# A two-dimensional FFT with a routed eight-expert network on one core: the order of the first thirteen steps and of the first weights

## The chip, the cores and the metric

The kernel runs on one core of a Trainium2 chip. The metric is the device time of one execution in microseconds (us). The engines are called PE (TensorE, matmuls), DVE (VectorE), ACT (ScalarE), POOL (GpSimd) and SP (SyncE, which issues most DMAs).

## The reference

```python
def _attn_ref(x):                       # x: 8 x 2496 x 256
    X = np.fft.fft(x, axis=1)
    X = np.fft.fft(X, axis=2)
    return X.real.astype(np.float32)

def _moe_ref(x, w_gate, w_output_gate, w1, w2):      # x: 19968 x 256, 8 experts, 256 -> 1024 -> 256
    logits = x @ w_gate
    e_idx = np.argmax(logits, axis=1)
...
    gate_w = probs[np.arange(N), e_idx]
    eom = 1.0 / (1.0 + np.exp(-(x @ w_output_gate)))
...
        h = np.maximum(x[mask] @ w1[e], 0.0)
        ye = h @ w2[e]
        out[mask] = gate_w[mask, None] * eom[mask, e, None] * ye
```

The real part of a two-dimensional FFT of each of 8 batches gives 19968 tokens of 256 numbers. Each token goes to the one of eight experts with the largest logit, through two matrix products with a ReLU between, and is scaled by two gates.

## The kernel before, in words

**FFT.** A batch comes in five chunks of 128 x 1024 floats (`xt`, 512 KB each, `load_x`, L302). `fold1` (L413) adds the two halves of a chunk; for batches from 3 on it makes two more half folds (L416, L417). `fold2` (L429, L432, L441, L443) makes sums and differences of the parts and frees the chunk, which starts the next `xt` load; ACT squares the result for the batch's energy (L451). `energy`, `energy_sum` and `scale` (L454 to L467, with the helper at L270) make a power of two from it. `dstage` (L482 to L486) is the first matrix product, in float32, five per batch. `devac` brings its result from PSUM as two half-precision parts, the high one on ACT (`ahi`, L494), the low one on DVE (`alo`, L495). The second product, `sstage` (L521), comes in five steps of 24, 24, 60, 36 and 36 matmuls per batch, so there are 40 steps n = 5b + i. `sevac` (L536 to L556) turns a step's result into rows of tokens: `qb`, `qs`, `eo`, `rt`, `rows`.

**Routing.** `gating(b)` is a generator in pieces "C" and "A" that computes logits, the expert and the destination of each token (`desti`), and then scatters the batch's rows to the buffer `scr` in memory with 20 indirect DMAs on POOL (L653). It yields after scatters 4, 9 and 14 (`SPL`), so that other POOL work comes between. `table_a(0)` makes the table of which expert serves which slot, for the tokens of batches 0 and 1 (`BAS[0]` = 2).

**Weights' scales.** 16 loads of 1 MB (`wt`, L363, two buffers) are squared on ACT (L367), summed by PE (L371), and give scales (`wscales`, and `ssc`, L715 to L717 per slot).

**Experts.** A slot is 256 tokens. `load_x_` reads its rows from `scr`, transposed (`xr`, L1075) and their two gates (`xf`, L1076). `load_w` reads its expert's weights as float32 halves (`raw0b`, `raw1b`, L1089); `conv` splits each into a high part on ACT (L1095) and a low part on DVE (L1096) and then issues the reload of that `raw` buffer for the next block. PE makes `hp` (L1115), ACT `hh` (L1119) and DVE `hl` (L1120) split it again, PE makes `yp` (L1135), ACT scales it (`y`, L1142), and POOL scatters it to the output (L1143).

**Order.** `start()` and `steps()` are the FFT's program. Up to step `FSTART` = 15 the program runs under `manual_schedule(engines=PH1)`: SP and POOL keep the written order, and a scheduler orders PE, DVE and ACT. Then the pools of the experts are opened, `table_a(0)` is made, and expert slots and the further FFT steps are interleaved (`rates`, `work`), in the same mode. Only the last part is fully in written order. A queue is served in order: an instruction that waits holds up all behind it on its engine.

## Time and profile before

| what | value |
|---|---|
| runs of the kernel before | 1174.66 us median of 3 (1174.36, 1174.66, 2767.52) |
| the profiled execution, own time | 1159.36 us |
| its span in the profile | 1157.5 us |
| its mean granted PE clock | 0.973 |
| PE busy, share of the span | 1052.7 us, 91% |
| DVE busy | 833.0 us, 72% |
| ACT busy | 731.6 us, 63% |
| POOL busy | 498.6 us, 43% |

The profile shows one execution; its times count from the start of the span. A row of the timeline gives start and duration in us, engine, line, operation, what is written from what, and in brackets the idle time before it and what ended it. A row of waits gives who waited for whom: us in total, how often, the longest. A row of groups gives a line's busy time, the mean of one in ns, and the idle time before it. A row of the stretches gives length and then busy time and instructions of PE, PEld (weight loads), DVE, ACT and POOL, the granted PE clock, the DMA engines' share and GB/s.

### The profile page before, as it was taken

What the parts mean: (1) busy time and instruction counts of PE and PEld (TensorE: products, weight loads), DVE (VectorE), ACT (ScalarE), POOL (GpSimd) and SP (SyncE); (2) the same over time, 40 slices, a digit from 0 to 9 for tenths busy, and PEclk for the clock granted to TensorE, in tenths of its full rate; (3) what the DMA queues carried; (4) which work ended last, traced back from release to release, by engine and by line L of the source; (5) the groups of instructions that cost most, each with busy time, mean ns of one, the idle gap of its engine ahead of it and who ended that gap; (6) DMA issues with size and microseconds to landing.
All of it is one profiled execution on the core that took longest, in us unless ns stands there. A gap on an engine that the chain in (4) does not pass through costs nothing.

```text
span 1157.5 us, 28573 instructions
## 1 busy us (share of the span) xinstructions
PE 1052.7 (91%) x10060; PEld 934.4 (81%) x10060; DVE 833.0 (72%) x1535; ACT 731.6 (63%) x1216; POOL 498.6 (43%) x430
## 2 busy tenths in 40 slices
PE   3877469989999999998999999999999989999998
PEld 3666458878788887887878888889989979998887
DVE  7876797878988747568445454588777867787684
ACT  2598657666666654553445454587777767777684
POOL 5418873786577444462564122223222322322231
PEclk9998779999999999999999999999999999999999
DMA  7778554755547545464767524557457464655651
GB/s 285 300 260 346 214 161 137 222 164 149 168 144 183 138 131 151 137 166 143 186 182 177 142 57 122 154 159 196 128 170 201 125 166 113 175 166 147 183 130 30
DMA packets 158213, 194.09 MB, mean 168 GB/s; under 512 B 117885, under 2 KB 118527, under 8 KB 156020
## 3 DMA queue, kind: packets, MB, share of 16 engines
q1 hardware_dynamic: 142100, 149.68, 46.6%
q0 software_dynamic: 15824, 42.14, 10.9%
q8 instruction: 79, 1.29, 0.5%
q14 instruction: 66, 0.54, 0.2%
q10 hardware_dynamic: 144, 0.44, 0.1%
HBM read 193.47 MB, written 43.46 MB: 205 GB/s over the span
## 4 chain that ended last, share of the span: by engine, by line
PE 63%; DVE 11%; issue 8%; POOL 6%; ACT 5%; DMA 3%; SPq 2%; another core or an unknown queue 0%; POOLq 0%; DVEq 0%; ACTq 0%
PE hp L1115 30%; PE yp L1135 29%; PE psb_t L521 3%; POOL scr L653 2%; POOL out_dram L1143 2%; DVE w1b L1096 1%; DVE rt L549 1%; DMA raw1b<-in_w_dram 1%; DVE hl L1120 1%; POOL xt L413 1%; SPq L1057 1%; ACT wt L367 1%; DVE w0b L1096 1%; DVE xt L432 1%; ACT w1b L1095 1%
## 5 line engine op out<-in xcount | busy, mean ns | idle before, releaser
L1115 PE MATMUL hp<-xr,w0b 128*128 128x256 f16 (+2 forms) x4224 | 482.8, 264 | 20.9 <-DVE hl L1120 13.7
L1135 PE MATMUL yp<-w1b,hh 128*128 128x256 f16 x2608 | 450.4, 273 | 6.7 <-issue 3.6
L1143 POOL DMA_INDIRECT out_dram<-y,xf x163 | 214.7, 1317 | 554.1 <-ACT y L1142 520.2
L1115 PEld LDWEIGHTS <-w0b 128*128 128x128 f16 x4224 | 384.6, 98 | 70.4 <-issue 15.4
L1135 PE MATMUL yp<-w1b,hl 128*128 128x256 f16 (+3 forms) x1304 | 356.0, 273 | 2.0 <-issue 2.0
L1135 PEld LDWEIGHTS <-hh 128*128 128x128 f16 x2608 | 251.9, 98 | 40.3 <-issue 11.9
L1119 ACT ACTIVATE hh<-hp 128x512 f16<-128x512 f32 (+4 forms) x352 | 194.0, 554 | 131.6 <-PE hp L1115 112.9
L1120 DVE SCALAR_TENSOR_TENSOR hl<-hp,hh 128x512 f16<-128x512 f32 (+4 forms) x352 | 222.0, 637 | 68.2 <-ACT hh L1119 56.9
L1096 DVE SCALAR_TENSOR_TENSOR w1b<-raw1b,ssc,w1b 128x1024 f16<-128x1024 f32 x144 | 186.3, 1294 | 111.7 <-ACT w1b L1095 90.3
L1096 DVE SCALAR_TENSOR_TENSOR w0b<-raw0b,ssc,w0b 128x1024 f16<-128x1024 f32 x144 | 190.2, 1324 | 69.6 <-ACT w0b L1095 51.7
L653 POOL DMA_INDIRECT scr<-rows,desti x160 | 178.6, 1116 | 73.3 <-issue 43.8
L1095 ACT ACTIVATE w0b<-raw0b,ssc 128x1024 f16<-128x1024 f32 x144 | 164.6, 1146 | 64.6 <-PE hp L1115 28.6
L1095 ACT ACTIVATE w1b<-raw1b,ssc 128x1024 f16<-128x1024 f32 x144 | 165.2, 1148 | 55.0 <-PE yp L1135 25.0
L1135 PEld LDWEIGHTS <-hl 128*128 128x128 f16 (+3 forms) x1304 | 127.9, 98 | 19.0 <-issue 4.2
L1142 ACT ACTIVATE y<-yp,ysc 128x256 f32<-128x256 f32 (+1 forms) x163 | 68.9, 470 | 43.4 <-PE yp L1135 34.2
L413 POOL TENSOR_TENSOR xt<-xt 128x500 f32<-128x500 f32 (+1 forms) x35 | 47.0, 1346 | 21.8 <-DMA xt<-in_xl_dram 19.5
L482 PE MATMUL psb_t<-tdet,ft 128*125 128x290 f32 (+1 forms) x120 | 36.2, 458 | 16.5 <-DVE alo L495 12.2
L482 PEld LDWEIGHTS psb_t<-tdet,ft 128*125 128x125 f32 (+1 forms) x120 | 24.7, 213 | 25.1 <-issue 13.5
L521 PE MATMUL psb_t<-ahi,tstq 125*128 125x145 f16 (+1 forms) x384 | 41.4, 227 | 3.3 <-DVE rt L539 2.0
L521 PEld LDWEIGHTS <-tstq 125*128 125x128 f16 (+1 forms) x576 | 38.6, 97 | 5.4 <-issue 4.6
L551 ACT CAST rows<-rt 128x516 f16<-128x516 f32 x40 | 25.0, 625 | 21.7 <-DVE rt L549 11.3
L484 PE MATMUL psb_t<-tdet,ft 128*125 128x145 f32 (+1 forms) x100 | 22.9, 313 | 16.8 <-DVE alo L495 9.4
(214 smaller groups left out, 916.4 us busy)
## 6 DMA issues: line engine op xcount, KB each, us to landing
raw0b<-in_w_dram SPq DMA_DIRECT2D x144, 512.0 KB
raw1b<-in_w_dram SPq DMA_DIRECT2D x144, 512.0 KB
xt<-in_xl_dram SPq DMA_DIRECT2D x40, 512.0 KB
wt<-in_w_dram SPq DMA_DIRECT2D x16, 1024.0 KB
out_dram<-y,xf POOLq DMA_INDIRECT x163
scr<-rows,desti POOLq DMA_INDIRECT x160
xr<-scr SPq DMA_TRANSPOSE x88
xf<-scr SPq DMA_DIRECT2D x75, 2.0 KB
```

Of the source, the lines that this page charges most:

```text
L413: eng.tensor_tensor(x0, x0, x1, op=ALU.add)
L482: nc.tensor.matmul(o[:, 0:290], ft[:, k, par, W], tdab[:, k], start=(k == 0), stop=(k == 1))
L521: nc.tensor.matmul(ps[:, k, c0:c0 + 145], tab[hl][t][K], a[K, kc, par, c0:c0 + 145], start=(n == 0), stop=(n == len(terms) - 1))
L653: free_order("scr", batch=b, inst=nc.gpsimd.indirect_dma_start(out=scr[:, :], out_offset=bass.IndirectOffsetOnAxis(ap=desti[:, j:j + 1], a ...
L1095: nc.scalar.activation(w[:, 0], r, AF.Copy, scale=sc)
L1096: nc.vector.scalar_tensor_tensor(w[:, 1], r, sc, w[:, 0], op0=ALU.mult, op1=ALU.subtract)
L1115: nc.tensor.matmul(ps[:, k, T], w1v[:, hl, kc, (f % 4) * 128:(f % 4 + 1) * 128], a["x"][:, x, T], start=(m == 0), stop=(m == 5))
L1119: nc.scalar.activation(hh[:, G, T], ps[:, :, T], AF.Relu)
L1120: nc.vector.scalar_tensor_tensor(hl[:, G, T], ps[:, :, T], 0.0, hh[:, G, T], op0=ALU.max, op1=ALU.subtract)
L1135: nc.tensor.matmul(a["yp"][0:M, u], a[k, h][:, f, u * 128:u * 128 + M], w2v[:, hl, f], start=(g == 0 and f == 0 and m == 0), stop=(h == 1 ...
L1142: nc.scalar.activation(a["y"][0:M, u], a["yp"][0:M, u], AF.Copy, scale=ys[0:M, u:u + 1])
L1143: free_order("out", nc.gpsimd.indirect_dma_start(out=out[:, :], out_offset=bass.IndirectOffsetOnAxis(ap=a["f"].bitcast(I32)[0:M, u, 1:2], ...
```

## The change

1. All folds of batches 0 to 2 (`fold1`, `fold2`) run on DVE; before, some ran on POOL.
2. `start()` is in written order on all engines, written anew, with table loads among the x loads; the first two `wt` loads come at its end.
3. The weight squares are spread to end by step 11 instead of 15.
4. At step 10 the whole of `gating(1)` is woven in at once, with its 20 scatters in a row (`SPL` counts only from batch 2 on), and `table_a(0)` up to its scales.
5. `FSTART` is 13 instead of 15. At step 12 the rest of the table is made, the experts' pools are opened, and the first four weight loads and `conv(0, 0, h)` come, with the reloads they issue, ahead of `load_x_(0)`. `hold` keeps batch 4's x loads back until then.
6. Batches 3's and 4's folds come later (`AHEAD`), and batch 3's five `dstage` calls stand at step 14 (`DSTEP`), with later energies (`ESTEP`).

The lines of the kernel change their numbers: fold1 L413 is L420, half folds L416/417 are L423/424, fold2 L429/432/441/443 are L435/438/447/449, `alo` L495 is L502, scatters L653 are L660, `conv` on DVE L1096 is L1128, `xr` L1075 is L1107, the raw loads L1089 are L1121, `hp` L1115 is L1147, `hl` L1120 is L1152.

```diff
@@ -63,11 +63,17 @@
 MARGIN = 2 + len(SPL)
-FSTART = 5 * BA + MARGIN
-W0, NW = 2, 2
-AHEAD = (5, 6, 7, 8, 9), (4, 5, 6, 7, 8)
+MARGIN0 = 3
+FSTART = 5 * BA + MARGIN0
+WEND, NW = FSTART - 1, 2
+AHEAD = {0: (5, 6, 7, 8, 9), BA - 1: (5, 5, 5, 5, 5), BA: (0, 1, 3, 5, 6)}
+AHEAD_ = (2, 4, 5, 5, 6)
+ESTEP = 1, 3, 2
+DSTEP = ((), (), (0, 1), (2, 3), (4,)), ((), (), (), (), (0, 1, 2, 3, 4)), ((), (), (), (0, 1, 2), (3, 4))
@@ -293,7 +299,7 @@
             while n and len(xq) < NB * KC:
-                q = pw if held[pw] < NX2 and len(xq) < FSTART + 8 else px
+                q = pw if held[pw] < NX2 and len(xq) < FSTART + 3 else px
                 if held[q] == (NX2 if q is pw else NX):
@@ -319,7 +325,7 @@
         nc.sync.dma_start(tdot, tdo)
-        load_x()
+        load_x(KC - 1)
@@ -379,6 +385,7 @@
         gens = []
+        first, hold = [], []
@@ -425,11 +432,10 @@
             v = xts[b, c].rearrange("p (h a b) n -> p h a b n", h=2, a=2)[:, h]
-            eng = nc.gpsimd if b < 2 and c in (2, 4) else nc.vector
-            eng.tensor_sub(ft[:, :, 1, W], v[:, :, 0, W], v[:, :, 1, W])
+            nc.vector.tensor_sub(ft[:, :, 1, W], v[:, :, 0, W], v[:, :, 1, W])
             yield
             e = v[:, :, 0]
-            eng.tensor_add(e[:, :, W], e[:, :, W], v[:, :, 1, W])
+            nc.vector.tensor_add(e[:, :, W], e[:, :, W], v[:, :, 1, W])
             if c in (0, 2):
@@ -444,7 +450,8 @@
                 held[xq[b * KC + k]] -= 1
-                load_x()
+                if not hold:
+                    load_x()
                 if b == 0:
@@ -657,7 +664,7 @@
                     scatter(j)
-                    if j in SPL:
+                    if j in SPL and b >= BA:
                         yield "C"
@@ -783,6 +790,7 @@
             yield
+            yield "scales"
             yield from slot_scales(ea, n, i)
@@ -930,52 +938,79 @@
         def start():
             gt_ = gate_tables()
-            next(gt_)
-            for c in range(KC):
-                fold1(0, c, nc.gpsimd if c % 2 else nc.vector)
-                if c == 2:
-                    for _ in gt_:
-                        pass
-                weave(fold2(0, c))
-                if c > 2:
-                    dstage(0, c - 3)
             for j in range(2):
                 load_t(j)
+                load_x(1)
+            def fold(c):
+                weave(fold2(0, c))
+            fold1(0, 0, nc.vector)
+            next(gt_)
+            fold(0)
+            fold1(0, 1, nc.vector)
+            for _ in gt_:
+                pass
+            fold(1)
+            for c in range(2):
+                dstage(0, c)
+            fold1(0, 2, nc.vector)
+            fold(2)
+            fold1(0, 3, nc.vector)
+            fold(3)
+            fold1(0, 4, nc.vector)
+            energy(0)
+            energy_sum(0)
+            dstage(0, 2)
+            for j in range(2, 4):
+                load_t(j)
+            fold(4)
             nc.sync.dma_start(tidt, tid)
                 nc.sync.dma_start(scr[DUM + 128 * k:DUM + 128 * (k + 1), :], ztile)
-            energy(0)
-            energy_sum(0)
+            for j in range(4, 6):
+                load_t(j)
             scale(0)
             for c in range(KC):
-                if c > 1:
-                    dstage(0, c)
                 devac(0, c)
+                if c < 2:
+                    dstage(0, c + 3)
+                if c == 2:
+                    fold1(1, 0, nc.vector)
+            for k in range(NW):
+                wload(k)
             wk = 0
-            fc = KC
+            fc = KC + 1
             for n in range(5 * NB):
                 b, i = divmod(n, 5)
+                late = int(b >= BA) + int(b > BA)
                 if i == 0 and b > 0:
                     add_gen(gating(b - 1))
+                    if b == BA:
+                        hold.append(1)
+                        for ph in "CACC":
+                            weave(piece(ph))
+                        first.append(table_a(0))
+                        while next(first[0]) != "scales":
+                            pass
                 smalls.clear()
-                ds_ = ((), (), (0, 1), (2, 3), (4,))[i] if b + 1 < NB else ()
+                ds_ = DSTEP[late][i] if b + 1 < NB else ()
                 for c in ds_:
                 fillers = [piece("C")]
-                for j in range(2, 6) if n == 0 else ():
-                    load_t(j)
-                while fc <= min(KC * (b + 1) + AHEAD[b >= BA][i], KC + 3 * n + 2):
+                while fc <= min(KC * (b + 1) + AHEAD.get(b, AHEAD_)[i], KC + 3 * n + 2):
                     m = fc
                     if m < NB * KC:
-                        fold1(*divmod(m, KC), nc.vector if m % KC == 1 and m // KC < 3 else nc.gpsimd)
+                        fold1(*divmod(m, KC), nc.vector if m // KC < 3 else nc.gpsimd)
                     if m - 1 < NB * KC and m > KC:
@@ -986,21 +1021,18 @@
                     pass
-                if i == 1 and b + 1 < NB:
+                if i == ESTEP[late] and b + 1 < NB:
                     energy(b + 1)
                 weave(piece("A"))
-                while wk <= 2 * E and wk < (n - W0 + 1) * (2 * E + 1) / (FSTART - W0):
+                while wk <= 2 * E and wk < (n + 1) * (2 * E + 1) / WEND:
                     if wk < 2 * E:
                     wk += 1
-                if n == W0 - 1:
-                    for k in range(NW):
-                        wload(k)
                 yield ("step", n)
@@ -1146,13 +1178,15 @@
         def experts():
-            chained(load_x_, 0)
             for m in range(2):
                     chained(load_w, 0, m, h)
-            chained(load_x_, 1)
             for h in range(2):
                 conv(0, 0, h)
+            yield "w"
+            chained(load_x_, 0)
+            hold.clear()
+            chained(load_x_, 1)
             yield "i"
@@ -1227,31 +1261,36 @@
+    with tc.manual_schedule():
+        start()
     with tc.manual_schedule(engines=PH1):
-        start()
         steps_ = steps()
         for m in steps_:
+            if m == ("step", WEND):
+                for _ in first[0]:
+                    pass
+                rp.close()
+                fx.append(pl(ctx, name="fr", bufs=2, side="right"))
+                add_raw(fx[0])
+                add_wbuf(fx[0])
+                fg = experts()
+                next(fg)
             if m == ("step", FSTART):
                 break
-        rp.close()
-        fx.append(pl(ctx, name="fr", bufs=2, side="right"))
         pps.close()
         pool["m"] = pl(pps, name="psm2", bufs=1, space=PS)
-        for _ in table_a(0):
-            pass
-        add_raw(fx[0])
-        add_wbuf(fx[0])
+        next(fg)
+        load_x()
         bg = background()
         ends = [n - 2 for n in range(1, NS) if sched[n][0] != sched[n - 1][0]]
-        work = [5 * (b - a) + 45 * C_TAB for a, b in zip(BAS, BAS[1:])] + [5 * (NB - BAS[-1]) - MARGIN + 28 * C_SCAT + 50 * C_TAB + 3.5]
+        work = [5 * (b - a) + (MARGIN - MARGIN0) * (i == 0) + 45 * C_TAB for i, (a, b) in enumerate(zip(BAS, BAS[1:]))] + [5 * (NB - BAS[-1]) - MARGIN + 28 * C_SCAT + 50 * C_TAB + 3.5]
         rates = [w / (9.0 * (e - s_)) for w, s_, e in zip(work, [0] + ends, ends)]
         acc, slot = 0.0, 0
-        fg = experts()
         for m in fg:
```

On **POOL**, from the first scatters on. `xt` are chunks, `rows` the tokens' rows of a step, `desti` a batch's destinations (its number tells the batch: the first is batch 0, the second batch 1). Before:

```order
L653 DMA scr_60<-rows_308,desti_791 161024x258 x4
L653 DMA scr_60<-rows_375,desti_791 161024x258
L413 TENSOR_TENSOR xt_496<-xt_496 128x4x125
L416 TENSOR_TENSOR xt_496<-xt_496 128x2x125
L417 TENSOR_TENSOR xt_496<-xt_496 128x2x125
L653 DMA scr_60<-rows_375,desti_791 161024x258 x3
L653 DMA scr_60<-rows_500,desti_791 161024x258 x2
L413 TENSOR_TENSOR xt_639<-xt_639 128x512
L416 TENSOR_TENSOR xt_639<-xt_639 128x256
L417 TENSOR_TENSOR xt_639<-xt_639 128x256
L653 DMA scr_60<-rows_500,desti_791 161024x258 x2
```

Of the change:

```order
L660 DMA scr_60<-rows_659,desti_794 161024x258 x4
L660 DMA scr_60<-rows_733,desti_1162 161024x258 x4
L660 DMA scr_60<-rows_796,desti_1162 161024x258 x4
L660 DMA scr_60<-rows_978,desti_1162 161024x258 x4
L660 DMA scr_60<-rows_1046,desti_1162 161024x258 x4
L660 DMA scr_60<-rows_1107,desti_1162 161024x258 x4
L420 TENSOR_TENSOR xt_384<-xt_384 128x4x125
L423 TENSOR_TENSOR xt_384<-xt_384 128x2x125
```

All 40 scatters of batches 0 and 1 stand in a row, and the folds of batch 3 (`xt_384`, `xt_504`, `xt_508`) and of batch 4's first chunks, which stood between them, stand behind.

On **DVE**, around the first conversion of weights (`w0b00`, `w0b01` are the two halves of the first product's weights). Before:

```order
L443 TENSOR_TENSOR ft_2654<-xt_1123,xt_1264 128x2x125
L1096 SCALAR_TENSOR_TENSOR w0b00_1783<-raw0b00_1779,ssc0_76,w0b00_1783 128x1024
L1096 SCALAR_TENSOR_TENSOR w0b01_1784<-raw0b01_1780,ssc0_76,w0b01_1784 128x1024
L539 SCALAR_TENSOR_TENSOR rt_2421<-psb_t_2201,qb_2422 128x2x129 x2
L1096 SCALAR_TENSOR_TENSOR w1b00_1785<-raw1b00_1781,ssc0_76,w1b00_1785 128x1024
```

Of the change:

```order
L435 TENSOR_TENSOR ft_1439<-xt_384 128x2x125
L438 TENSOR_TENSOR xt_384<-xt_384 128x2x125
L447 TENSOR_TENSOR ft_1342<-xt_374,xt_384 128x2x125
L449 TENSOR_TENSOR ft_1439<-xt_374,xt_384 128x2x125
L435 TENSOR_TENSOR ft_1441<-xt_504 128x2x125
L438 TENSOR_TENSOR xt_504<-xt_504 128x2x125
L435 TENSOR_TENSOR ft_1608<-xt_508 128x2x125
L1128 SCALAR_TENSOR_TENSOR w0b00_1479<-raw0b00_1475,ssc0_76,w0b00_1479 128x1024
L438 TENSOR_TENSOR xt_508<-xt_508 128x2x125
L1128 SCALAR_TENSOR_TENSOR w0b01_1480<-raw0b01_1476,ssc0_76,w0b01_1480 128x1024
```

The half folds of batch 3's chunks 1, 2 and 3, whose folds POOL makes behind the last scatter, stand ahead of the conversion.

On **SP**, around the first load of tokens. Before:

```order
L302 DMA xt_1692<-in_xl_dram 128x1024
L1057 TENSOR_LOAD slots_a0_69
L1057 ISA x2
L1075 ISA
L1075 DMA_TRANSPOSE xr_1796<-scr_60 128x4x256
```

Of the change:

```order
L1121 DMA raw0b00_1475<-in_w1_dram 128x1024
L1089 TENSOR_LOAD slots_a0_69
L1089 ISA x2
L1089 TENSOR_LOAD slots_a0_69
L1089 ISA x2
L1121 ISA
L1121 DMA raw0b01_1476<-in_w1_dram 128x1024
L1089 TENSOR_LOAD slots_a0_69
L1089 ISA x2
L1107 ISA
L1107 DMA_TRANSPOSE xr_1671<-scr_60 128x4x256
```

These are the reloads of the `raw` buffers for the second block, which `conv` issues; they wait for the conversions and now stand ahead of the first `xr`. On PE, steps 14 to 17 and eight `dstage` calls, which stood ahead of the first `hp`, stand behind it.

## The prediction

> **What bounds the kernel now.** I read the page's totals and chain first, then the waits of the first 170 us, then busy time by stretch, last the timeline around the scatters and the first expert matmul.
>
> ```profile
> span 1157.5 us, 28573 instructions
> PE 1052.7 (91%) x10060; PEld 934.4 (81%) x10060; DVE 833.0 (72%) x1535; ACT 731.6 (63%) x1216; POOL 498.6 (43%) x430
> PE 63%; DVE 11%; issue 8%; POOL 6%; ACT 5%; DMA 3%; SPq 2%; another core or an unknown queue 0%; POOLq 0%; DVEq 0%; ACTq 0%
> ```
>
> TensorE (PE) is busy 1052.7 of 1157.5 us, so about 105 us of idle is all that any reordering can win. DVE stands second in the chain. Where the idle lies, the waits of the first 170 us tell:
>
> ```profile
> POOL scr L653 <- ACT qs L537: 26.3, 1, 26.3
> PE psb_t L482 <- DVE alo L495: 12.2, 3, 9.4
> PE psb_t L484 <- DVE alo L495: 9.4, 1, 9.4
> PE psm_t L371 <- ACT wt L367: 8.4, 1, 8.4
> ```
>
> POOL had nothing to do for 26.3 us before the first scatter, and PE stood still for DVE's `alo` and for ACT's weight squares. Busy time by stretch (columns: length, then PE, PEld, DVE, ACT, POOL, then granted clock, DMA share, GB/s):
>
> ```profile
> 60.00:80.00 20.00, 15.10 (x170) 13.10 (x168) 17.66 (x61) 20.00 (x41) 0.00 (x0) 1.00 0.72 272
> 80.00:160.00 80.00, 48.52 (x422) 43.87 (x422) 59.33 (x183) 54.15 (x109) 66.39 (x65) 0.79 0.68 248
> 177.30:228.80 51.50, 48.39 (x471) 43.34 (x469) 42.31 (x72) 34.71 (x59) 30.35 (x26) 1.00 0.59 178
> 228.80:298.90 70.10, 62.16 (x621) 55.22 (x619) 57.89 (x138) 45.68 (x86) 52.84 (x46) 1.00 0.56 162
> 298.90:362.60 63.70, 59.67 (x589) 53.71 (x588) 55.37 (x101) 42.10 (x76) 39.74 (x35) 1.00 0.64 172
> ```
>
> Between 80 and 160 us POOL is the full engine (66.39 of 80) and PE is idle for 31.5 us. The last three rows are expert slots 0 to 12, each edge being the first `hl` of slot 0, 4, 8 and 12. There PE is busy 48.39 + 62.16 + 59.67 = 170.2 of 185.3 us, and DVE 42.31 + 57.89 + 55.37 = 155.6, or 84%. So two regimes matter: until 177.3 us a serial chain through DVE, ACT and POOL sets the time; behind it PE does, with DVE close by.
>
> **The change, part by part.** *First scale.* The chain starts with batch 0's folds, its scale and the first evictions.
>
> ```profile
> 7.72 0.68 DVE L413 TENSOR_TENSOR xt<-xt 128x500 f32<-128x500 f32 x1 [2.38 <-ACT sq L410]
> 11.95 0.67 DVE L413 TENSOR_TENSOR xt<-xt 128x500 f32<-128x500 f32 x1
> 19.71 1.72 DVE L413 TENSOR_TENSOR xt<-xt 128x500 f32<-128x500 f32 x1
> 24.50 2.85 DVE L432 TENSOR_TENSOR xt<-xt 128x250 f32<-128x250 f32 x2
> 28.99 0.15 DVE L270 TENSOR_SCALAR p_x<-psm_t 128x1 int32<-128x1 int32 x1
> 29.74 0.42 DVE L432 TENSOR_TENSOR xt<-xt 128x250 f32<-128x250 f32 x1
> ```
>
> The same fold takes 0.67 us alone and 1.72 us with POOL folding beside it, the same half fold 0.42 and 1.43. With POOL out, DVE has 5 folds at 0.67, 16 half folds at 0.42 and some ten gate-table instructions, about 2.4 us: 3.4 + 6.7 + 2.4 = 12.5 us, so the scale comes at 7.7 + 12.5 = 20.2 us, against 28.99. The last chunk had landed by 19.71 at the latest; behind that stand one fold and four half folds, 2.4 us, so 22.1 is the upper bound.
>
> *First scatter and last scatter.*
>
> ```profile
> 80.69 1.14 POOL L653 DMA_INDIRECT scr<-rows,desti  x1 [26.30 <-ACT qs L537]
> 85.99 0.97 POOL L653 DMA_INDIRECT scr<-rows,desti  x1 [0.30 <-issue]
> 86.98 1.27 POOL L413 TENSOR_TENSOR xt<-xt 128x500 f32<-128x500 f32 x1
> 88.33 0.71 POOL L416 TENSOR_TENSOR xt<-xt 128x250 f32<-128x250 f32 x1
> 89.00 0.72 POOL L417 TENSOR_TENSOR xt<-xt 128x250 f32<-128x250 f32 x1
> ...
> 103.77 2.34 POOL L653 DMA_INDIRECT scr<-rows,desti  x1 [0.30 <-issue]
> ...
> 113.34 0.97 POOL L653 DMA_INDIRECT scr<-rows,desti  x1 [0.30 <-issue]
> ...
> 121.11 1.00 POOL L653 DMA_INDIRECT scr<-rows,desti  x1 [1.34 <-issue]
> ...
> 155.44 0.98 POOL L653 DMA_INDIRECT scr<-rows,desti  x1 [0.30 <-issue]
> ```
>
> From scale to first scatter took 80.69 - 28.99 = 51.7 us. In that stretch the change takes work from POOL to DVE and starts the weight squares sooner; ACT, already full in 60:80, gets about two more of these before the first scatter, while DVE loses its contended folds. I know neither to better than 5 us and keep 51.7: first scatter at 72 us (67 to 77). Then 40 scatters stand on POOL without a fold between. Batch 1's 20 took 156.4 - 121.1 = 35.3 us with three fold groups of 2.7 to 3.4 us in it, so 1.30 us each: 40 x 1.30 = 52 us. Batch 1's destinations must be there at 72 + 26 = 98 us; I allow 2 us for waiting. Last scatter ends at 126 us (119 to 133), against 156.4.
>
> The Trainium skill ("SBUF — State Buffer", section "A bandwidth-pool intuition that's wrong (but worth ruling out)") speaks against this packing: an indirect DMA that GpSimd prepares waits while DVE holds the port that both share, about 3100 instead of 620 ns beside DVE copies. The trace so far does not bear it out: DVE was busy 59.33 of these 80 us, and the scatters quoted kept 0.97 to 1.14 us but for one of 2.34. By the rule at its worst the 40 would take an estimated 40 x 3.4 = 136 us instead of 52, by the rows they stay at 52.
>
> *From the last scatter to the first `hl`.* Here the order costs something. Three fold groups of batch 3 now stand behind the last scatter on POOL; DVE's half folds of these stand ahead of the conversion of the first weights; SyncE's reload of `raw0b` waits for that conversion and stands ahead of the first `xr` load.
>
> ```profile
> 157.98 1.35 SPq L1075 DMA_TRANSPOSE xr<-scr  x1
> 160.81 1.50 SPq L1089 DMA_DIRECT2D raw0b<-in_w_dram  x2
> 166.44 1.28 DVE L1096 SCALAR_TENSOR_TENSOR w0b<-raw0b,ssc,w0b 128x1024 f16<-128x1024 f32 x1
> 167.36 0.23 PE L521 MATMUL psb_t<-ahi,tstr 125*128 125x145 f16 x1
> 169.27 0.46 PE L484 MATMUL psb_t<-tdet,ft 128*125 128x145 f32 x2
> 170.03 0.60 PE L1115 MATMUL hp<-xr,w0b 128*128 128x256 f16 x4
> 177.33 1.28 DVE L1120 SCALAR_TENSOR_TENSOR hl<-hp,hh 128x512 f16<-128x512 f32 x2
> ```
>
> Before: last scatter 156.4 to first `hl` 177.33, 20.9 us. After: three groups at 2.75 are 8.3; two half folds and two conversions, 2 x 0.42 + 2 x 1.28, are 3.4; the reloads 1.5; `xr`, 1.35 to issue and an estimated 2 to land; from first `hp` to first `hl` an estimated 5.5 (7.3 before, with FFT work between). Sum 22 us. The first weights are loaded and half converted long before, but this buys nothing, since the last of the conversion hangs on POOL. First `hl` at 126 + 22 = 148 us: **29 us earlier**.
>
> *What is given back.* Nothing was deleted, so work left undone by the first expert matmul comes later. On PE these are steps 14 to 17, 36 + 24 + 24 + 60 = 144 matmuls, and eight `dstage` calls. From 167.36 to 169.27 us stand 30 such matmuls, 0.064 each, and one `dstage` lasts 169.27 to 170.03, 0.76: 9.2 + 6.1 = 15.3 us. On DVE I count 382 instead of 307 instructions in slots 0 to 12:
>
> ```profile
> L552 DVE TENSOR_TENSOR rows<-rt,rows 128x516 f16<-128x516 f32 x12 | 8.3, 689 | 0.1
> L545 DVE SCALAR_TENSOR_TENSOR eo<-psb_t,qb 128x290 f32<-128x290 f32 x20 | 8.2, 450 | 2.0 <-ACT qb L543 2.0
> L549 DVE TENSOR_TENSOR rt<-eo 128x258 f32<-128x258 f32 x18 | 7.4, 449 | 0.1
> L495 DVE SCALAR_TENSOR_TENSOR alo<-psb_t,p_x,ahi 125x580 f16<-125x580 f32 x9 | 7.1, 812 | 0.0
> L429 DVE TENSOR_TENSOR ft<-xt 128x250 f32<-128x250 f32 x10 | 4.2, 418 | 11.3 <-POOL xt L417 11.3
> ```
>
> Eight more `alo` at 0.81 (6.5), four `eo` and six `rt` at 0.45 (4.5), four `rows` at 0.69 (2.8), twelve half folds at 0.42 (5.0), and some 41 small ones, most of a further gating round, at least 0.15 each (6.2): 25 us. DVE then has 155.6 + 25 = 180.6 us to do. If PE alone decides, slots 0 to 12 grow by PE's 15.3 us; if DVE keeps its share of 84%, they last 180.6 / 0.84 = 215, or 29.7 more.
>
> ```profile
> PE hp L1115 <- DVE hl L1120: 6.0, 7, 1.5
> ```
>
> DVE has room above 84%, but PE needs its `hl` in between and already waits 6.0 us for it in 177 to 363; I take the middle, **22 us more**, at which DVE would be 87% busy. Behind slot 12 the two orders nearly meet again; I add 1 us.
>
> *The rest.* Weight squares moved forward cost nothing as long as their loads hide behind the 0.7 DMA share of 60:160; uncovered they would hold up the table, and with it the slots, but that table now stands behind a chain 50 us long. Batch 4's x loads, held back to stand behind `xr`, are first needed in the slots.
>
> **Sum:** -29 + 22 + 1 = -6 us. The profiled execution took 1159.36 us (span 1157.5 and 1.9 around it), 15.3 under the median 1174.66 shown, of three runs; by the sum it would be 1153.4. I put the 6 us on the median: 1168.7.
>
> **Rivals.** *(A) DVE isn't the limit.* Then the slots give back only PE's 15.3 us, and if the first scatter also comes at 67 us, the last ends at 121: -34 + 15.3 + 1 = -18, 1157. With 126 it is -13, 1162. For it: the 6.0 us of waits for `hl` are few; against: 84% is an average, and in slots 4 to 8 PE had 7.9 us of idle at DVE's 83%.
>
> *(B) Slower: late folds starve DVE.* The change folds batch 4 later, so the half folds come nearer to POOL's folds. Already 11.3 us of DVE's idle in slots 0 to 12 is a half fold waiting for POOL (the `L429` row), with conversions and `hl` queued behind it. If that doubles and the folds beside them widen DVE's, its share falls to 80%: 180.6 / 0.80 = 225.8, 40.5 more, -29 + 40.5 + 1 = +12.5, 1187. Break-even is a give-back of 28 us, a share of 84.7%: the case decides below that.
>
> *(C) The scatter chain does not come earlier.* If ACT, not DVE, sets the first scatter, it stays near 80.7; without folds between, the last then ends at 134.7, the first `hl` comes at 156.7, 20.6 earlier, and with 22 + 1 given back nothing is left: +2.4, 1177. For it: ACT's 20.00 of 20 in 60:80. Against: DVE's 17.66 there and the 9 us saved ahead of it.
>
> *(D) Scatters stretched by DVE.* If each of the 40 took the 2.34 us of the longest quoted, 1.35 more than most, that is 54 us, which the packing would keep whole: 1168.7 + 54 = 1223. It decides from a spacing of 1.5 us. For it is that one row, against it all others. (The Trainium skill's rule named above would be this case.)
>
> **How the numbers follow.** Forecast 0.47, (A) 0.24, (B) 0.16, (C) 0.10, (D) 0.03. The forecast's own range is -13 to +2, 1162 to 1177. For eight in ten I reach into (A) to 1148 (both its gains and 4 us more on the first scatter, or a lower share of waits) and to (B)'s 1187. Over 2% is 23.5 us, about what a measurement of this kernel can tell from no change: faster than 1151.2 is the outer half of (A) with the forecast's tail, 0.15; slower than 1198.2 is (D) with the tail of (B), 0.06; the rest 0.79.
>
> **What would show it.** Right, step by step: scale of batch 0 (`p_x`, 128x1) at 20 to 22 us; first scatter at 67 to 77; 40 scatters with 1.3 us between starts, ending at 119 to 133; POOL's three fold groups right behind, then the `w0b` conversion, reload, `xr`; first `hl` at about 148 with PE idle for some 20 us ahead of it; first `hl` of slot 12 about 207 us later, DVE 85 to 89% busy in between. Wrong: a first scatter still at 80, scatters of 2 us and more, or slots 0 to 12 done in 201 us or less (A), or in 213 and more (B). If the first `hl` comes before 140 us, I have mis-seen the chain behind the scatters.

## The result, and the profile after

The changed kernel took 1202.62 us (median of 4 runs, 1201.34 to 1205.54), the kernel before 1174.51: a ratio of 1.0274, 95% interval 1.0243 to 1.0304. (One run of the kernel before took 2767.52 us; the ratio leaves such slow runs out, and the two medians alone give 1.024.) It is slower by 2.7%, where 6 us faster was forecast. Three more comparisons of the same two kernels, on three chips, gave 1.0295 (1.0233 to 1.0357), 1.0295 (1.0278 to 1.0312) and 1.0291 (1.0257 to 1.0324). Its profiled execution took 1205.54 us. From the page of the change:

```profile
span 1203.7 us, 28571 instructions
PE 1064.1 (88%) x10060; PEld 939.2 (78%) x10060; DVE 847.1 (70%) x1553; ACT 732.5 (61%) x1216; POOL 479.6 (40%) x412
PE 61%; issue 12%; DVE 8%; POOL 7%; DMA 5%; ACT 4%; SPq 2%; another core or an unknown queue 2%; POOLq 0%; ACTq 0%; DVEq 0%
```

PE does the same 10060 matmuls, so the 46.2 us between the spans are 11.4 us more of busy time (1064.1 against 1052.7) and 34.8 us more of idle. The medians lie only 28.1 us apart: the profiled execution of the kernel before was 15 us under its median, that of the change 3 us over its own, so the two profiles show more than the typical loss. Where it arises, the stretches tell: up to the first `hp`, on to the first `hl` of slot 12, on to that of slot 32, and the rest. Before:

```profile
0.00:170.03 170.03, 106.13 (x896) 92.21 (x897) 134.43 (x352) 108.53 (x226) 104.76 (x105) 0.85 0.71 262
170.03:362.60 192.57, 177.48 (x1756) 159.21 (x1754) 160.37 (x315) 128.84 (x230) 122.94 (x105) 1.00 0.61 169
362.60:626.50 263.90, 247.95 (x2330) 218.02 (x2328) 164.28 (x394) 134.93 (x240) 132.35 (x119) 0.99 0.58 156
626.50:1157.50 531.00, 521.13 (x5085) 464.95 (x5083) 373.89 (x478) 359.35 (x522) 138.56 (x101) 1.00 0.54 143
```

After:

```profile
0.00:165.16 165.16, 79.19 (x654) 66.22 (x655) 103.01 (x285) 93.42 (x183) 60.71 (x64) 0.78 0.66 244
165.16:396.90 231.74, 209.89 (x1972) 187.14 (x1973) 199.48 (x391) 144.53 (x266) 143.49 (x122) 0.93 0.55 157
396.90:675.20 278.30, 255.10 (x2353) 221.85 (x2351) 170.53 (x403) 135.42 (x245) 137.51 (x126) 0.96 0.59 150
675.20:1203.70 528.50, 519.90 (x5086) 463.97 (x5084) 374.08 (x478) 359.11 (x522) 137.88 (x101) 1.00 0.54 143
```

The first `hp` comes 4.9 us earlier, but with 26.9 us less of PE's work done (79.19 against 106.13): PE's idle ahead of it grew from 63.9 to 86.0 us. The next two stretches have 6.8 and 7.3 us more of idle, and in them the granted clock is 0.93 and 0.96 instead of 1.00 and 0.99.

The waits of the first 200 us name the idle times:

```profile
POOL scr L660 <- ACT qs L544: 19.3, 1, 19.3
POOL scr L660 <- ACT wt L373: 18.2, 1, 18.2
PE hp L1147 <- DMA xr<-scr: 40.8, 1, 40.8
PE psb_t L528 <- issue: 13.7, 12, 2.4
```

PE waits 40.8 us in one piece for the first tokens, and POOL 18.2 us in the middle of its scatters. The scatters, first and last of each batch:

```profile
74.95 1.18 POOL L660 DMA_INDIRECT scr<-rows,desti  x1 [19.29 <-ACT qs L544]
...
99.59 0.98 POOL L660 DMA_INDIRECT scr<-rows,desti  x1 [0.30 <-issue]
118.75 0.99 POOL L660 DMA_INDIRECT scr<-rows,desti  x1 [18.18 <-ACT wt L373]
...
144.79 0.98 POOL L660 DMA_INDIRECT scr<-rows,desti  x1 [0.30 <-issue]
```

The second batch's destinations were not there at 100.6. (The row names a weight square on ACT that ended at the same moment; `desti` is written on DVE at 117.1 us, and the gates in `rows` until 118.5.) Why, PE's timeline shows: these are the products of one FFT step, some 0.064 us apart in the prediction's rows.

```profile
90.74 0.28 PE L528 MATMUL psb_t<-ahi,tstq 125*128 125x145 f16 x1 [0.46 <-issue]
92.14 0.29 PE L528 MATMUL psb_t<-alo,tstq 125*128 125x145 f16 x1 [1.12 <-issue]
93.58 0.28 PE L528 MATMUL psb_t<-ahi,tstq 125*128 125x145 f16 x1 [1.15 <-issue]
94.98 0.28 PE L528 MATMUL psb_t<-ahi,tstq 125*128 125x145 f16 x1 [1.12 <-issue]
...
103.54 0.45 PE L528 MATMUL psb_t<-ahi,tstq 125*128 125x145 f16 x2
```

From 86.8 to 103.5 us PE has 16 matmuls in 16.7 us and waits for no semaphore that the profile shows. The stretch begins near the tenth scatter of the row that starts at 74.95 and ends 3 us behind its last. ACT and DVE, which evict that step, all but stand still with it (2.00 and 0.00 us busy). A smaller one, 226.8 to 233.7 us, lies in a row of ten scatters (219.8 to 232.8).

The rest of the early chain, on DVE:

```profile
20.87 0.15 DVE L276 TENSOR_SCALAR p_x<-psm_t 128x1 int32<-128x1 int32 x1
156.06 1.74 DVE L1128 SCALAR_TENSOR_TENSOR w0b<-raw0b,ssc,w0b 128x1024 f16<-128x1024 f32 x1
168.58 0.68 DVE L1152 SCALAR_TENSOR_TENSOR hl<-hp,hh 128x512 f16<-128x512 f32 x1
```

The scale came at 20.87 (forecast 20.2), the first scatter at 74.95 (72), the first `hl` 22.8 us behind the last scatter (22).

### The profile page after: what moved, and what is told of

Its sections match the earlier page's. It is cut to its first block, busy times and chain, and to the rows that moved or that the text cites. A ratio compares the mean times of both kernels' runs of the same rounds, so it can differ in the third digit from the quotient of the medians.

```text
span 1203.7 us, 28571 instructions
## 1 busy us (share of the span) xinstructions
PE 1064.1 (88%) x10060; PEld 939.2 (78%) x10060; DVE 847.1 (70%) x1553; ACT 732.5 (61%) x1216; POOL 479.6 (40%) x412
## 3 DMA queue, kind: packets, MB, share of 16 engines
q8 instruction: 79, 1.29, 0.5%
## 4 chain that ended last, share of the span: by engine, by line
PE 61%; issue 12%; DVE 8%; POOL 7%; DMA 5%; ACT 4%; SPq 2%; another core or an unknown queue 2%; POOLq 0%; ACTq 0%; DVEq 0%
PE hp L1147 28%; PE yp L1167 28%; POOL scr L660 3%; PE psb_t L528 3%; POOL out_dram L1175 1%; DMA wt<-in_w_dram 1%; DMA xt<-in_xl_dram 1%; DVE w1b L1128 1%; DVE ft L435 1%; DVE hl L1152 1%; POOL xt L420 1%; ACT wt L373 1%; PE psb_t L493 1%; DMA scr<-rows,desti 1%
## 5 line engine op out<-in xcount | busy, mean ns | idle before, releaser
L1147 PE MATMUL hp<-xr,w0b 128*128 128x256 f16 (+2 forms) x4224 | 494.5, 267 | 69.4 <-DMA xr<-scr 40.8
L1147 PEld LDWEIGHTS <-w0b 128*128 128x128 f16 x4224 | 388.2, 99 | 126.2 <-issue 67.5
L1152 DVE SCALAR_TENSOR_TENSOR hl<-hp,hh 128x512 f16<-128x512 f32 (+4 forms) x352 | 222.2, 637 | 71.4 <-ACT hh L1151 64.4
L1128 DVE SCALAR_TENSOR_TENSOR w1b<-raw1b,ssc,w1b 128x1024 f16<-128x1024 f32 x144 | 189.0, 1313 | 108.6 <-ACT w1b L1127 91.9
L1128 DVE SCALAR_TENSOR_TENSOR w0b<-raw0b,ssc,w0b 128x1024 f16<-128x1024 f32 x144 | 190.9, 1328 | 70.4 <-ACT w0b L1127 50.9
L660 POOL DMA_INDIRECT scr<-rows,desti x160 | 174.9, 1093 | 85.8 <-issue 44.5
L420 POOL TENSOR_TENSOR xt<-xt 128x500 f32<-128x500 f32 (+1 forms) x25 | 33.7, 1346 | 59.8 <-DMA xt<-in_xl_dram 59.6
L528 PEld LDWEIGHTS <-tstq 125*128 125x128 f16 (+1 forms) x576 | 41.9, 101 | 19.2 <-issue 18.1
L528 PE MATMUL psb_t<-ahi,tstq 125*128 125x145 f16 (+1 forms) x384 | 45.6, 236 | 9.4 <-issue 9.4
L552 DVE SCALAR_TENSOR_TENSOR eo<-psb_t,qb 128x290 f32<-128x290 f32 x64 | 26.3, 450 | 32.8 <-ACT qb L550 29.9
L528 PE MATMUL psb_t<-alo,tstq 125*128 125x145 f16 (+1 forms) x192 | 40.1, 234 | 6.7 <-issue 6.7
L458 ACT ACTIVATE sq<-ft 128x500 bf16<-128x500 f32 (+1 forms) x35 | 21.8, 622 | 36.0 <-DVE ft L447 31.3
```

The lines of the kernel that those rows point to most:

```text
L420: eng.tensor_tensor(x0, x0, x1, op=ALU.add)
L528: nc.tensor.matmul(ps[:, k, c0:c0 + 145], tab[hl][t][K], a[K, kc, par, c0:c0 + 145], start=(n == 0), stop=(n == len(terms) - 1))
L660: free_order("scr", batch=b, inst=nc.gpsimd.indirect_dma_start(out=scr[:, :], out_offset=bass.IndirectOffsetOnAxis(ap=desti[:, j:j + 1], a ...
L1128: nc.vector.scalar_tensor_tensor(w[:, 1], r, sc, w[:, 0], op0=ALU.mult, op1=ALU.subtract)
L1147: nc.tensor.matmul(ps[:, k, T], w1v[:, hl, kc, (f % 4) * 128:(f % 4 + 1) * 128], a["x"][:, x, T], start=(m == 0), stop=(m == 5))
L1152: nc.vector.scalar_tensor_tensor(hl[:, G, T], ps[:, :, T], 0.0, hh[:, G, T], op0=ALU.max, op1=ALU.subtract)
```

## The experiments

Theory 1: the unbroken rows of scatters slow PE's issue. Theory 2: batch 3's folds, now behind the scatters, leave PE without work ahead of the first `hp`. Rivals: the slow stretch is an accident; the slots lose through DVE, or through the late places of later products and folds. Each ratio is to the kernel before on the same chip. There are two conditions: beside some of these kernels before took 1160 to 1175 us (slower condition), beside others 1132 to 1135 (faster condition), so only ratios within one condition are compared. Times in an expectation that was meant for the other condition say little; its ratios and the order of events count.

**The same kernel again** (e1; e10 and e18 were further ones).

> The changed kernel itself once more, for a second profile. Theory 1 (bursts): twenty scatters without a break on POOL slow PE's issue, as in the first profile, where PE issued one matmul every 1.1 to 1.4 us from 86.8 to 103.5 us while scatters ran from 75.0 to 100.6; so the slow stretch comes again, 8 us or more of PE idle before 106 us, and scatter 21 starts 10 us or more after scatter 20. Rival (give-back): that stretch was one execution's accident; scatter 21 starts within 3 us of scatter 20, and the time is 1198 to 1206 us all the same, because the work left behind the first expert matmul makes it.

Ratio 1.0295. The stretch came again, 87.2 to 103.0 us, scatter 21 at 119.50. In all four profiles of the change it stands at 87 to 103. It is no accident.

**Scatters in fives** (e2).

```diff
-                    if j in SPL and b >= BA:
+                    if j in SPL:
```

> The change, but the scatters of batches 0 and 1 are given out after the fifth, tenth and fifteenth again, with fold groups between. Theory 1: no slow stretch of PE above 4 us before 110 us, batch 1's scatters start by 112 us, the last ends at 138 to 146, and with folds of batch 3 done between, the first hl comes at 155 to 160: 1185 to 1195 us. Rival: the fold groups only lengthen the scatter chain by some 8 us, the last ends at 150 or later: 1200 to 1210 us.

Ratio 1.0217 (1.0155 to 1.0279), 10 us under the change (1187.11 against 1197.05). But not as theory 1 had it: no POOL work falls between the first batch's scatters in that program, so its row stayed unbroken and the stretch stayed (85.3 to 101.8). The gain goes with folds of batch 3 that now stand between the second batch's scatters: the first `hl` came at 161.8 (e1: 170.0) although the last scatter ended only at 153.5.

**Memsets between fives** (e3; a cut of the edit, `GAPN` is 5).

```diff
+                    if j in SPL and b < BA:
+                        for _ in range(GAPN):
+                            nc.gpsimd.memset(dmy, 0.0)     # dmy: an unused 128 x 512 tile
```

> The change, with five small memsets of an unused tile on POOL after the fifth, tenth and fifteenth scatter of batches 0 and 1 and no other move; the memsets are additional work, the outputs are the same. Theory 1, if it is the unbroken row that counts: the slow stretch of PE is under 6 us, batch 1's destinations come by 110 us, and the time falls by 5 to 15 us, to 1188 to 1197, although POOL does more. Rival: POOL's row gets longer by the six gaps, some 10 to 15 us, and the time rises to 1205 to 1215. If it is POOL's total of scatters that counts and not the row, the slow stretch stays and the time is 1200 to 1210.

Ratio 1.0215 (1.0148 to 1.0282). The same stretch of time in the change's second profile and here:

```profile
86.00:104.00 18.00, 6.04 (x31) 3.42 (x31) 0.49 (x2) 2.94 (x4) 10.94 (x12) 0.64 0.62 218
```

```profile
86.00:104.00 18.00, 14.47 (x190) 12.77 (x188) 11.54 (x36) 13.80 (x25) 14.96 (x20) 1.00 0.86 290
```

and its scatter 21, the first of batch 1:

```profile
109.59 0.99 POOL L662 DMA_INDIRECT scr<-rows,desti  x1 [0.30 <-issue]
```

190 matmuls instead of 31, at a clock of 1.00 instead of 0.64, and scatter 21 starts with no wait. Nothing but idle work on POOL was added, so theory 1 is shown for this stretch. The kernel as a whole gained 8.5 us, 0.8 points of the 3.0. That is not the price of the stretch: the memsets lengthen POOL's chain (last scatter at 143.9, in e1 at 146.5), so the first `hl` came only 2.5 us earlier (167.5), and where the other 6 us were gained is not shown.

**Two more steps ahead of the experts** (e4; further lines of the edit keep the first weights and the first loads of tokens in their places).

```diff
-MARGIN0 = 3
+MARGIN0 = 5
```

> The change, but two more FFT steps (13 and 14, with the five float32 products of batch 3) stand ahead of the interleaving with the experts, as before the change; the first loads of tokens keep their place. Theory 1: PE's slow stretch and the late second batch of scatters stay (last scatter at 145 us), and some 10 us of PE work moves into PE's 40 us of idle before the first hp: 1190 to 1198 us. Rival (give-back): this is the main loss, and 15 us or more come back: 1188 us or less.

Ratio 1.0342 (1.0275 to 1.0409): no gain, and both expectations missed. The first `hl` moved to 189.7 us. The added steps need batch 3's folds, which stand behind the last scatter (144.7), so PE could not use its idle time for them. This fits theory 2, seen from the other side.

The next four ran in the faster condition (before: 1134.68 us).

**One part alone: rows of twenty in the kernel before** (e5).

```diff
-                    if j in SPL:
+                    if j in SPL and b >= BA:
```

> The kernel before with one part of the change alone: the scatters of batches 0 and 1 are given out twenty in a row, the fold groups that stood between them come behind. Theory 1 (bursts): PE gets a slow stretch of 8 us or more within the first row of scatters, as the change had from 86.8 to 103.5 us, and the time rises by 8 to 20 us, to 1168 to 1180 (before: 1160). Rival: the slow stretch belongs to the new start and its order; here PE's pauses in the first 120 us stay under 4 us and the time within 4 us of before.

Ratio 1.0121 (1.0092 to 1.0150). PE was idle only 2.5 us (98.0 to 104.0) and 4.1 us (139.9 to 145.7), which the profile puts down to waits, not to issue, and yet the time rose by 12.9 us, as theory 1 had it without its cause: the first `hl` came at 185.3 us. Neither expectation holds whole.

**The other early part alone: the new start and folds on DVE** (e6: `start()` of the change, `fold1` and `fold2` of batches 0 to 2 on `nc.vector`, in the kernel before).

> The kernel before with the other early part alone: the new start in written order, and all folds of batches 0 to 2 on DVE; scatters, weight squares, steps and the first weights as before the change. Theory 1: this part is good, scale of batch 0 near 21 us, first scatter 4 to 9 us earlier than 80.7, and the time 2 to 8 us below before, 1152 to 1158. Rival (folds on DVE make the rest late): 1163 us or more.

Ratio 0.9976 (0.9959 to 0.9993), first scatter at 78.78 us: this part is good by 2.7 us, at the small end, and the first scatter came less early than the 4 us expected.

**The old places of later products and folds** (e7).

```diff
-DSTEP = ((), (), (0, 1), (2, 3), (4,)), ((), (), (), (), (0, 1, 2, 3, 4)), ((), (), (), (0, 1, 2), (3, 4))
+DSTEP = (((), (), (0, 1), (2, 3), (4,)),) * 3
-ESTEP = 1, 3, 2
+ESTEP = 1, 1, 1
-AHEAD = {..., BA: (0, 1, 3, 5, 6)}          AHEAD_ = (2, 4, 5, 5, 6)
+AHEAD = {..., BA: (4, 5, 5, 5, 6)}          AHEAD_ = (4, 5, 6, 7, 8)
```

> The change, but with the old places of the float32 products and energies for all batches and the folds from batch 4 on as early as before the change; batch 3's folds still stand behind the 40 scatters. Theory 2 (the first hp finds PE without work because batch 3's folds stand behind the scatters): this hardly helps, 1190 to 1200 us (the change: 1197). Rival (B of the prediction: folds and products placed later starve DVE and PE in the slots): slots 12 to 32 shrink from about 207 or 214 us to 203 or less, slots 0 to 12 by 10 or more, and the time is 1183 or less.

Ratio 1.0193 (1.0167 to 1.0219). In this condition the row of scatters did not slow PE at all:

```profile
97.72 0.98 POOL L660 DMA_INDIRECT scr<-rows,desti  x1 [0.30 <-issue]
102.85 1.45 POOL L660 DMA_INDIRECT scr<-rows,desti  x1 [4.16 <-issue]
```

The last scatter ended at 128.95, within the 119 to 133 forecast for the change, and the kernel was still 1.9% slower. So the slow stretch is not the main loss there. What PE waited for instead, the chain of batch 3's first fold shows, behind the last scatter on POOL, then on DVE, then on PE:

```profile
128.96 1.26 POOL L420 TENSOR_TENSOR xt<-xt 128x500 f32<-128x500 f32 x1
131.72 1.44 DVE L435 TENSOR_TENSOR ft<-xt 128x250 f32<-128x250 f32 x1 [19.03 <-POOL xt L424]
134.99 0.82 PE L491 MATMUL psb_t<-tdet,ft 128*125 128x145 f32 x2 [36.96 <-DVE ft L447]
```

PE stood still for 37 us because batch 3's products need these folds.

**Batch 3's folds back between the scatters** (e9).

```diff
-                    if j in SPL and b >= BA:
+                    if j in SPL:
-BA - 1: (5, 5, 5, 5, 5), BA: (0, 1, 3, 5, 6)}
+BA - 1: (5, 6, 7, 8, 9), BA: (4, 5, 5, 5, 6)}
-DSTEP = ..., ((), (), (), (), (0, 1, 2, 3, 4)), ...          ESTEP = 1, 3, 2
+DSTEP = ..., ((), (), (0, 1), (2, 3), (4,)), ...          ESTEP = 1, 1, 2
```

> The change with batch 3's folds back between the scatters: scatters of batches 0 and 1 in fives, folds of batch 3 in steps 5 to 9 and its float32 products at steps 12 and 13. The early start, the paced weight squares, the first weights split early and the later batches' new places stay. Theory 2: PE has batch 3's products to do while it waits, 7 us of PE work or more stand ahead of the first hp, DVE's conversion no longer hangs on POOL, first hl at 150 to 160 us, and together with shorter scatter rows 20 to 30 us come back: 1167 to 1177 us. Rival (the slots themselves are the loss): 1185 us or more, slots 0 to 12 still 220 us.

Ratio 0.9932 (0.9908 to 0.9957): 0.7% faster than before. PE up to the first `hp`, in the kernel just told and in this one:

```profile
0.00:161.54 161.54, 89.69 (x734) 77.61 (x735) 107.09 (x298) 96.31 (x187) 58.27 (x64) 0.81 0.69 249
```

```profile
0.00:145.79 145.79, 100.64 (x839) 87.61 (x839) 109.16 (x313) 100.07 (x200) 65.57 (x70) 0.88 0.78 287
```

The first `hp` comes 15.8 us earlier and with 11 us more of PE's work behind it. 1156.17 against 1126.68 us, 29.5 us, and PE's wait of 37 us is gone. This shows theory 2 in the faster condition, for the folds together with the fives that let them in: the two were not separated there. The kernels also differ in the late places, but e15 and e16 below, which differ in these alone, lie 1.9 us apart.

The next three ran beside e10, the change again, in the slower condition (before: 1170.05 us).

> The changed kernel a third time, beside the three kernels below and against before on the same chip, since two chips gave before 1160 and 1135 us and in one kernel with twenty scatters in a row, timed on the faster chip, PE had no slow stretch. Theory 1 (the row slows PE's issue) in its strict form: a slow stretch of 8 us or more again within the first row. Theory 1 in the weaker form, that it takes a second thing that differs by chip: on the faster chip no such stretch, last scatter near 129 us as forecast, and the change still 1.5 to 2.5% slower than before, because batch 3's folds stand behind the scatters; on the slower chip the stretch and 2.5 to 3.5%.

Ratio 1.0295, stretch at 86.7 to 102.9 us: the weaker form.

**Batch 3's folds early, but scatters in rows of twenty** (e11: as e9, without the first edit).

> As the kernel before last with batch 3's folds in steps 5 to 9 and its float32 products at steps 12 and 13, but each batch's twenty scatters in one row: two fold groups of batch 3 stand between the two rows. Theory 2 (batch 3's folds behind the scatters are the main loss): nearly all of the gain stays, ratio to before 0.99 to 1.01, first hl within 5 us of the kernel with fives (150.6). Rival (unbroken rows are the main loss): ratio 1.015 or more.

Ratio 1.0213 (1.0193 to 1.0232). The rival's ratio holds in this condition. Each row now has its slow stretch, PE with 19 and 12 matmuls in 18 us:

```profile
88.00:106.00 18.00, 4.21 (x19) 1.62 (x19) 3.02 (x6) 3.80 (x7) 14.39 (x16) 0.57 0.61 215
128.90:147.10 18.20, 3.04 (x12) 1.16 (x12) 0.00 (x0) 2.00 (x2) 14.65 (x16) 0.57 0.55 212
```

**Batch 3's folds early, fives, and the old late places** (e12: e9 and e7 together).

> The kernel with batch 3's folds between scatters in fives, and in addition the old places of the products, energies and folds of the batches from 4 on. Theory: these late places cost or bring little, within 4 us of the kernel without (ratio 0.993): 0.989 to 0.997. Rival: the later folds of batch 4 on starve DVE in the slots; then slots 0 to 12, 205 us with the new places, shrink to 195 or less and the ratio is 0.985 or less.

Ratio 1.0016 (0.9997 to 1.0034), 2 points under e11, from which it differs in the fives and in the late places. Neither expectation. Slots 0 to 12 took 205 us. A row of twenty formed across the two batches (97.2 to 123.5 us), and with it a stretch, 114.1 to 126.0.

**Less DVE work in the slots** (e13). Slots 2 to 11 leave out the low part of the weights; the products use an older one.

```diff
-            nc.vector.scalar_tensor_tensor(w[:, 1], r, sc, w[:, 0], ...)
+            if not 2 <= n < 12:
+                nc.vector.scalar_tensor_tensor(w[:, 1], r, sc, w[:, 0], ...)
```

> The change, but in slots 2 to 11 DVE leaves out the low part of the weights (40 instructions of 1.28 us, some 51 us of DVE's work), which stays that of an earlier slot; PE, ACT, loads and order are the same. If DVE bounds the slots 0 to 12, as the prediction's 22 us of give-back took it, they shrink by 12 us or more, to 215 or less (the change: 227 to 228), with PE's half clock gone. Rival (PE's moved work and its waits for other things set them): within 5 us of the change.

Ratio 1.0302 (1.0283 to 1.0321), the change beside it 1.0295. Slots 0 to 12, of e10 and of this kernel:

```profile
169.20:396.30 227.10, 202.75 (x1954) 181.48 (x1953) 197.03 (x383) 143.13 (x263) 143.21 (x122) 0.96 0.57 158
```

```profile
169.60:398.50 228.90, 201.86 (x1927) 179.28 (x1926) 146.50 (x342) 141.52 (x263) 122.81 (x121) 0.95 0.55 157
```

DVE's busy time, the third of the five, fell from 197.03 to 146.50 us, and the slots took 228.9 instead of 227.1. So the amount of DVE's work is not what sets them. The test has a limit: PE's waits for DVE in these slots fell from 13.4 to 6.8 us, while its pauses put down to issue rose from 8.9 to 18.4, so in these two profiles a gain of some 10 us could lie hidden behind the slowed issue.

**Four runs on what was open** (e14 to e17) fell into the faster condition (before: 1131.56 us), where no stretch appears, so what they say of it is little.

> The kernel before with the scatters of batches 0 and 1 in rows of twenty, once more, since its first run was on a chip on which no kernel showed PE's slow stretch (ratio there 1.012). If the rows alone make the stretch on the other chips: 8 us or more of pauses of PE within a row and a ratio of 1.015 or more. Rival (the stretch needs the changed start too): pauses under 5 us and again 1.008 to 1.015, from the folds that stand behind the rows.

1.0151 (1.0125 to 1.0177), no pause put down to issue in the rows: whether rows alone slow PE in the old start in the slower condition stays open.

> The kernel with batch 3's folds early, scatters in fives and the old late places (ratio 1.002 on a chip with the slow stretch, which it had from 114.1 to 126.0 us, where a row of twenty had formed across the two batches), with five memsets of an unused tile on POOL after every fifth scatter of batches 0 and 1. Theory 1: no slow stretch, 5 to 12 us less, ratio 0.990 to 0.997. Rival (POOL's longer chain costs as much): 1.000 to 1.006.

1.0085 (1.0055 to 1.0116), above the range of the rival too.

> The kernel with batch 3's folds between scatters in fives and the later batches' new places (ratio 0.993 on the chip without a slow stretch), with the same memsets after every fifth scatter of batches 0 and 1. Theory 1: no slow stretch before 150 us on any chip and a ratio of 0.985 to 0.998. Rival: 1.000 or more.

1.0062 (1.0037 to 1.0087), against 0.9932 without memsets: where there is no stretch to remove, the memsets only lengthen POOL's chain (last scatter at 158.98 us instead of 140.93), and that costs 1.3 points. The rival holds. e15 and e16 differ in the late places alone, 1140.64 against 1138.75 us: in this condition these places cost nothing.

> The change with the memsets only after the tenth scatter of batches 0 and 1, so rows of ten; the memsets are additional work. In all slow stretches so far PE slowed about 12 us after a row began, near its tenth scatter. If it is the row's length: pauses under 4 us before 110 us, second batch's scatters by 108 us, and the time 0.5 to 1.2% below the change (ratio 1.017 to 1.025). Rival (rows of ten are long enough): a slow stretch of 5 us or more remains, ratio 1.025 to 1.032.

1.0170 (1.0144 to 1.0196). That is the lower end of the range, but it says nothing on the length of a row, since nothing stalled. It shows once more 1.7% of loss with no slow stretch, in the change but for two gaps.

**The change and the kernel of e9, side by side** (e18 and e19, slower condition, before: 1171.87 us).

> The changed kernel a fourth time. Where before takes about 1132 us and no kernel shows the slow stretch: ratio 1.015 to 1.025, last scatter at 126 to 132 us, so the folds behind the scatters are the whole loss. Where before takes 1160 us or more: the slow stretch again and a ratio near 1.03.

1.0291, stretch at 88.1 to 103.4 us.

> The kernel with batch 3's folds between scatters in fives and the later batches' new places, again (0.993 where before took 1135 us). Where before takes about 1132 us: 0.990 to 0.996 again. Where before takes 1160 us or more: between 0.995 and 1.010, since a row of some fifteen scatters forms across the two batches and can bring the slow stretch; 20 us or more under the change in either case.

1.0117 (1.0088 to 1.0147), 20.8 us under the change, with a row of twenty across the two batches (100.4 to 127.0) and its stretch:

```profile
118.70:129.10 10.40, 1.54 (x7) 0.50 (x5) 3.39 (x10) 0.98 (x3) 8.49 (x10) 0.65 0.61 201
```

A little over the expected range. So this version beats both kernels in the faster condition and loses to the kernel before in the slower; e12 is level with it there. No version tried beats both kernels in both.

## Why the prediction was wrong, point by point

- **The sum** was -29 + 22 + 1 = -6 us. In the two profiles it is -8.7 to the first `hl`, +43.0 in slots 0 to 12, +14.4 in slots 12 to 32 and -2.5 behind: +46.2.
- **The early start** held: scale 20.87 against 20.2, first scatter 74.95 against 72, scatters 1.29 us apart. Alone it is worth 0.24% (e6).
- **The last scatter** failed: 145.8 against 126. The sentence "I allow 2 us for waiting" for batch 1's destinations is the step; POOL waited 18.2. I took PE's steps ahead of it as undisturbed by the row of scatters. e3 shows that the row itself held PE up. Where it did not (e7), POOL waited 4.2 us and the last scatter came at 128.95.
- **The rule on scatters beside DVE** (the Trainium skill, "SBUF — State Buffer", the section named in the prediction) did not act here: 0.98 us is what most scatters of the unbroken rows took, in e7 also beside a DVE that was busy 14.76 of the 18 us from 86 to 104. In rival (D) I had the row as the risk, but with POOL as the one that suffers; PE did.
- **Last scatter to first `hl`** held as a sum, 22.8 against 22, and the path was right: folds, half folds, conversion, reload and `xr`. That the sum fits so well is luck, since its terms missed both ways. The DVE part up to the end of the second conversion took 6.4 us instead of 3.4 (the first conversion 1.74 us, not 1.28), and first `hp` to first `hl` 3.4 instead of the 5.5, for which no row stood. The 2 us for `xr` to land had no row either and came out at 2.1.
- **PE's moved work** was sized at 15.3 us and is some 22.8. The step is "one `dstage` lasts ... 0.76". A call is two such groups, as rows of the changed kernel's timeline show:

```profile
171.21 0.41 PE L491 MATMUL psb_t<-tdet,ft 128*125 128x145 f32 x2
171.46 0.34 PE L492 MATMUL psb_t<-tdot,ft 128*125 128x80 f32 x2
171.64 0.45 PE L493 MATMUL psb_t<-tdot,ft 128*125 128x145 f32 x2
171.92 0.41 PE L491 MATMUL psb_t<-tdet,ft 128*125 128x145 f32 x2
172.17 0.34 PE L492 MATMUL psb_t<-tdot,ft 128*125 128x80 f32 x2
172.35 0.45 PE L493 MATMUL psb_t<-tdot,ft 128*125 128x145 f32 x2
```

  In slots 0 to 12 stand 36 more each of L491, L492 and L493, which is nine calls at 1.42 us, 12.8 us, and 156 more products of steps at 0.064, 10.0 us (forecast: eight calls and 144).
- **The give-back** was 43 us in slots 0 to 12 (168.6 to 396.9 is 228.3, before 185.3), not 22. I had reasoned through DVE's share and taken the middle of two bounds. DVE's share, 86.5%, was near the 87% forecast, but that is luck: its work grew by 42 us (197.5 against 155.6), not by 25, in slots that grew twice as much as forecast. By e13 the amount of that work is not the cause. By count, PE's own work and clock make up most of it. The three stretches of slots 0 to 12, after:

```profile
168.60:248.50 79.90, 71.20 (x661) 64.73 (x659) 63.90 (x122) 47.93 (x88) 38.64 (x35) 0.91 0.49 151
248.50:327.70 79.20, 71.80 (x695) 63.91 (x694) 69.93 (x134) 49.61 (x93) 53.96 (x45) 0.94 0.52 148
327.70:396.90 69.20, 63.45 (x603) 55.99 (x602) 63.69 (x131) 45.68 (x83) 50.88 (x44) 0.95 0.66 176
```

  PE is busy 206.45 us in them, 36.2 more than before, and idle 6.8 more. Of the 36.2, the moved work is some 22.8. The rest, 13.4, goes with the clock, which the prediction left out: clocks of 0.91, 0.94 and 0.95 make an estimated 31 us at half clock in these slots. No run tests this part alone. Two of the stretches at half clock:

```profile
229.40:240.00 10.60, 7.42 (x49) 7.18 (x49) 3.31 (x4) 2.97 (x4) 2.75 (x3) 0.52 0.24 90
287.40:294.00 6.60, 5.33 (x25) 4.06 (x26) 6.60 (x19) 4.69 (x10) 5.38 (x5) 0.50 0.61 184
```

  Both follow pauses of PE; before the change slots 0 to 12 had a clock of 1.00 throughout. (The Trainium skill, "TensorE: Matmul & The Clock Gate", Part 1: "The HAM clock gate", has the clock at half after an idle window of some 3.4 us. The trace agrees only in part: PE was idle for 3.4 us from 285.3 us on, but the clock fell some 2 us into that idle time, and at 229.4 us it fell while PE still had a matmul every 1.4 us, with no pause above 1.14.)
- **Behind slot 12** 1 us was forecast; slots 12 to 32 took 14.4 us more (278.3 against 263.9), 7.3 of it idle. The four profiles of the change have 271 to 284 us there, so the size is uncertain. They took 240 to 244 us in every profile of the faster condition, the ones of the change's order too, so the order is not enough to explain it. What the two conditions are stays open, but the profiles show how they differ: in these slots PE's pauses put down to issue, the kind of the slow stretch, come to 11.7 us in the kernel before, to 15.2 in the change and to 7.9 to 16.9 in all profiles of the slower condition; in the faster there are none. The largest row of the kernel before:

```profile
PE yp L1135 <- issue: 5.7, 11, 0.9
```

  In the slower condition, e12 with the old late places had ratio 1.0016 and e19 with the new 1.0117, not taken side by side; that these places cost 1 point there is likely, not shown.
- **The rivals.** The sign was (B)'s and the time beyond its 1187, but its mechanism, DVE starved by late folds, did not act. It asked that DVE's 11.3 us of waiting for POOL's folds in slots 0 to 12 double. In the change they are:

```profile
DVE ft L435 <- POOL xt L424: 1.8, 2, 1.3
```

  (C) did not occur.

Put together: the change starts the experts 5 to 9 us earlier and leaves 27 us of PE's work behind, because the work that could fill PE's wait hangs on folds that stand behind 40 scatters on POOL. In the faster condition that is the whole loss and more (e7 1.0193, e9 0.9932). In the slower, the row's stall comes on top, and moving the folds alone brings 0.8 points (e11 1.0213 against 1.0295); with fives and the old late places the rest is gone (e12 1.0016), and how it divides between these two is not shown. Why PE's issue slows beside the row is not shown either: it waits for no semaphore, and the profile calls it issue.
